# Up units of batch 0 taken by quarters of w1 over three token groups, with four moves in the loads and the fp32 bias table around them

## The chip, the cores and the metric

The kernel runs on one core of a Trainium2 chip. The time is device microseconds of one execution of the whole program, and less is better. The profile is one more execution, recorded by the hardware profiler; its times are counted from the start of its span.

## The reference

Two parts run one after the other. The first is attention over 4 batches of 8 heads, 768 positions and head dimension 64, with a bias that falls with distance, a causal window of 96 keys and 8 global keys:

```python
scores = scale * np.matmul(q, k.transpose(0, 1, 3, 2))
keep = is_global | is_local          # key < 8, or 0 <= query - key < 96
scores = np.where(keep, scores - slope[h] * dist, -1e9)
x = softmax(scores) @ v              # 4 x 768 x 512 after the heads are joined
```

The second is a mixer on x. U is 768x32, V is 32x768, w1 is 512x2048 and w2 is 2048x512:

```python
h = x.transpose(0, 2, 1) @ U @ V
u = x + h.transpose(0, 2, 1)
out = u + np.maximum(u @ w1, 0.0) @ w2
```

All inputs and the output are fp32 in memory; the kernel's matmuls take fp16, and bf16 for the bias on the tensor engine.

## The kernel before

**Work units.** Heads are taken in pairs, four pairs to a batch, so there are 16 pairs. For a pair the kernel loads q and k (`load_qk`, two transfers on the SP queue) and v (`load_v`, one), turns them to fp16 (`cast_qk`, `cast_v`, mostly on GpSimd), transposes q and k on the tensor engine (`st_T`, L239), copies the shifted keys (`st_KA`, `st_A`, `st_P`), makes the scores of three column chunks (`scores`, L339 and L346), adds the bias, takes the exponent and multiplies with v (`st_V`). A key block's scores cover two query blocks, one on the diagonal and one beside it.

**Two ways to add the bias.** For the four pairs of batch 0 (pairs 0 to 3) the tensor engine adds it, from a bf16 table `rel16` (L331), and ScalarE takes the exponent straight from PSUM (`st_SE`). From pair 4 on VectorE does it in `s_dve` (L371), from the fp32 table `relcat`, and ScalarE takes the exponent afterwards (`st_E`, L383). `relcat` is copied from `relB` by two ScalarE instructions (L733, L734), and its first eight rows are finished on GpSimd by `finish_table` (L184, L185). This stands late in the program, after pair 3's `st_V`.

**The mixer.** `st_M1` (U, L436 for batch 0) and `st_M2` (V and the identity, L453 and L458) build the transposed u in `uT`, one 128-column piece per pair. Then come up units and down units. An up unit (L582) multiplies two 128-column pieces of w1 with 256 tokens of `uT` into one PSUM bank, 8 matmuls, and ScalarE takes the relu into `htr` (L587). A batch has three token groups of 256, so 24 up units. The banks of the up units have the tag `th`, three buffers, which the transposes of `st_T` use as well. A down unit (L612) multiplies `htr` with w2.

**What sets the order.** The program is written out by hand: each engine runs its own instructions in program order. The queues `ups_q` and `downs_q` hold closures; `fill(n)` takes n units out of them at fixed places between the steps of a pair, and `unit` chooses whether an up or a down is next. `held` keeps the downs back until pair 7; by then pairs 4, 5 and 6 have taken eight up units each, all of batch 0. Before the first of them, two up units are begun with three of their four matmul pairs (`begin_up`, L502).

**The weights.** w1 is loaded by four transfers on the GpSimd queue (`load_w1`, L211), one for every 512 columns, a quarter; each casts fp32 to fp16 on the way. Up units 0 and 1 of a group need quarter 0, units 2 and 3 quarter 1, and so on. w2 follows in four more (`load_w2`, L214). U and V are loaded on the same queue during the setup (L197, L198).

**Loads of pairs.** SP issues, in this order: q and k of pairs 0 and 1, v of 0, q and k of 2, v of 1, q and k of 3, v of 2, v of 3, q and k of 4, q and k of 5, v of 4, q and k of 6, v of 5, q and k of 7, and so on. A buffer of q or k is that of the pair two before.

Of the kernel before, what the change touches and what calls it, by code (L numbers as in the profile page):

```python
# [20 lines left out]
def kernel(  # L21
# [13 lines left out]
    nc = tc.nc  # L35
# [3 lines left out]
    P = 128  # L39
# [52 lines left out]
    NVB = 4  # L92
    vbuf = [cst.tile([P, NSB, 2, D + 1], FP16, name=f"v16_{i}") for i in range(NVB)]

    def load_qk(i):
        b, h0 = i // NP, 2 * (i % NP)
        got = []
        for src, nm in ((q, "qst"), (k, "kst")):
            st = stp.tile([P, 2, NSB, D], FP32, name=nm, tag=nm, bufs=2)
            if i < NPE:  # L100
                nc.sync.dma_start(
                    st.rearrange("p h n d -> p h (n d)"),
                    src[b, h0:h0 + 2].rearrange("h (p n) d -> p h (n d)", n=NSB),
                )
            else:
                nc.sync.dma_start(
                    st.rearrange("p h n d -> p (h n) d"),
                    src[b, h0:h0 + 2].rearrange("h (n p) d -> p (h n) d", p=P),
                )
            got.append(st)  # L110
        staged[i] = got
# [82 lines left out]
    finish_table(rel16.rearrange("p a c -> p (a c)"), rel16[0:NG, :, P:])  # L194
    for t in (u16.rearrange("p n c -> p (n c)"), v16w):
        nc.gpsimd.memset(t.bitcast(I32), 0)
    nc.gpsimd.dma_start(u16[:, :, 0:R], moe_U.rearrange("(c p) r -> p c r", p=P))  # L197
    nc.gpsimd.dma_start(v16w[0:R], moe_V)  # L198
    for vt in vbuf:
        nc.gpsimd.memset(vt[:, :, :, D:D + 1], 1.0)  # L200

    w1_16 = wbig.tile([P, NDC, DFF], FP16, name="w1_16")
    w2_16 = wbig.tile([P, NJC, DM], FP16, name="w2_16")
# [333 lines left out]
    def queue_last_weight_sum():  # L537

        b12, b22 = quarters[1], quarters[3]
        for k, js in enumerate((slice(0, HJ // 2), slice(HJ // 2, HJ))):  # L540
            queue_sum("t3", k, b12[:, js], b22[:, js], b12[:, js], ALU.subtract)

    def queue_ff(b):
        for g in range(NFG):
            queue_group(b, g)

    def queue_group(b, g):
        ts = slice(g * FT, (g + 1) * FT)
# [23 lines left out]
        def mk_up(at):  # L572
            jp = at // 2 + (at % 2) * NJC // 4 if split else at

            def go():
                if jp == 0:
                    cell["htr"] = ffp.tile([P, NJC, FT], FP16, name="htr", tag="htr", bufs=3)
                hps, done = begun.pop(jp) if jp in begun else (ps_th("hps"), 0)
                for k in range(2):
                    jt = 2 * jp + k  # L580
                    for dc in range(done, NDC):
                        nc.tensor.matmul(  # L582
                            hps[:, k * FT:(k + 1) * FT],
                            w1_16[:, dc, jt * P:(jt + 1) * P], uT[:, dc, ts],
                            start=(dc == 0 and k == 0), stop=(dc == NDC - 1 and k == 1),
                        )
                nc.scalar.activation(  # L587
                    cell["htr"][:, 2 * jp:2 * jp + 2].rearrange("p j t -> p (j t)"), hps, AF.Relu
                )
                if split and at % 4 == 3:  # L590
                    queue_sums(at // 4)
            return go
# [46 lines left out]
                    store(*what)  # L639
            return go  # L640

        for at in range(NJC // 2):
            ups_q.append((mk_up(at), (b, g)))
        if split:
            x1 = mk_product("cx", lo, "a11", "b11", (n0, lo), first=True)
            x2 = mk_product("cx", lo, "s2", "t2", (n0, hi_))
# [18 lines left out]
                jobs.popleft()()  # L665

    def unit():
        down = downs_q and not held[0] and not any(w == downs_q[0][1] for _, w in ups_q)
        room = ups_q and (not downs_q or place(ups_q[0][1]) - place(downs_q[0][1])
                          < (3 if held[0] else 2))  # L670
        if down and (ahead[0] > 0 or not room):
            ahead[0] = 0
            downs_q.popleft()[0]()
        elif room:
            ahead[0] = 1
            ups_q.popleft()[0]()
# [11 lines left out]
    for i in range(NP):  # L688
        st_SE(i, 0)
        if i:  # L690
            st_V(i - 1, 0)
        cast_v(i)
        st_A(i)
        if i < 2:
            load_v(i + 2)
        if i in (1, 2):
            load_qk(NP - 1 + i)
        if i == 2:
            load_w1(0)
        if i == 3:  # L700
            load_v(NP)
        if i >= 2:
            st_M1(i - 2)
        if i:
            st_T(i + 1)
        st_SE(i, 1)
        if i:
            st_V(i - 1, 1)
        else:
            st_T(i + 1)  # L710
        st_KA(i + 1, nc.vector)
        st_P(i)
        if i == 2:
            st_M2(i - 2)
        if i == 0:
            cast_qk(i + 2, nc.vector, nc.gpsimd)
        elif i < 3:
            cast_qk(i + 2, nc.gpsimd)
        if i == 2:
            load_w1(1)  # L720
        if i == 3:
            load_w1(2)
            load_w1(3)
        st_SE(i, 2)
        if i == 3:
            st_M2(i - 2)
# [3 lines left out]
    st_V(NP - 1, 1)  # L730
    cast_qk(NP + 1, nc.gpsimd)
    st_M2(NP - 2)
    nc.scalar.copy(relcat[:, 0:512].rearrange("p (a c) -> p a c", a=2), rel3[:, 0:2])  # L733
    nc.scalar.copy(relcat[:, 512:640], relB[:, 0:P])  # L734
    finish_table(
        relcat, relcat[0:NG, 0:512].rearrange("p (a c) -> p a c", a=2)[:, :, P:]
    )
    begin_up(0, (0, 1), ps_cps("hps"))
    st_M1(NP - 1)
    begin_up(0, (2,))  # L740
# [1 line left out]
    st_M2(NP - 1)  # L742
    for xo, o, rb in later:
        nc.vector.tensor_tensor(xo, o, rb, ALU.mult)
    for hi in range(2):
        s_dve(NP, hi, first[hi])
    queue_ff(0)

    for i in range(NP, NPAIR + 2):
# [113 lines left out]
```

## Time and profile before

| what | us |
|---|---|
| median of 3 runs before | 236.97 (236.11 to 237.56) |
| the profiled execution's own time | 236.67 |
| its span, first to last instruction | 234.8 |
| VectorE busy | 151.4 (65%) |
| ScalarE busy | 112.2 (48%) |
| GpSimd busy | 80.3 (34%) |
| the SP and GpSimd queues together | 36.66 MB in 86561 packets |

In the rows that the prediction shows, PE is the tensor engine and PEld its weight loads, DVE is VectorE, ACT is ScalarE, POOL is GpSimd, and SPq is the queue from which SyncE issues transfers. A row of the timeline has the start, the time taken, the engine, the line, the operation, out<-in, the number of instructions merged into the row, and in brackets the idle time of the engine before it with what ended it. A DMA row on POOL or SPq is the issue alone; the transfer itself goes on afterwards. In a view of DMA packets by queue, q1 is the queue of SP and q0 that of GpSimd.

### The profile page before, as it was taken

How to read it: one execution, taken by the hardware profiler on the slowest of the kernel's cores; microseconds unless marked ns; L12 is line 12 of the kernel's file. 1: busy time of each engine (PE TensorE's matmuls, PEld its weight loads, DVE VectorE, ACT ScalarE, POOL GpSimd, SP SyncE). 2: the span in 40 equal slices, each digit the busy share in tenths (PEclk: the TensorE clock that was granted, in tenths of full speed). 3: DMA queues.
4: the chain of work that ended last, by engine and by line, in shares of the span. 5: the costliest groups of instructions: out<-in, count | busy, mean ns of one | idle time of the engine just before them, and what ended most of it. 6: DMA issues, size and time to landing. Idle time of an engine off the chain costs nothing.

```text
span 234.8 us, 5675 instructions
## 1 busy us (share of the span) xinstructions
PE 224.0 (95%) x2324; PEld 161.4 (69%) x2324; DVE 151.4 (65%) x349; ACT 112.2 (48%) x169; POOL 80.3 (34%) x128
## 2 busy tenths in 40 slices
PE   7989977999999999999999999999999999999994
PEld 2445755778844446876666656766688988888883
DVE  3677866468686777566667576779896543454452
ACT  6767765767714040837372626464542334334320
POOL 7379938294562432333333333302311100000000
PEclk9999999999999999999999999999999999999999
DMA  6999999999969798979695956362130302011112
GB/s 194 304 287 263 266 234 226 263 230 185 208 61 234 209 226 210 247 154 229 149 240 133 250 143 176 70 173 77 29 82 36 90 0 92 1 47 45 45 47 89
DMA packets 86561, 36.66 MB, mean 156 GB/s; under 512 B 74152, under 2 KB 83592, under 8 KB 86536
## 3 DMA queue, kind: packets, MB, share of 16 engines
q1 hardware_dynamic: 81480, 32.01, 55.6%
q0 software_dynamic: 5056, 4.29, 11.4%
q8 instruction: 18, 0.29, 0.5%
q14 instruction: 7, 0.06, 0.1%
HBM read 27.46 MB, written 6.29 MB: 144 GB/s over the span
## 4 chain that ended last, share of the span: by engine, by line
PE 77%; POOL 7%; DMA 7%; DVE 3%; ACT 1%; issue 1%; SPq 0%; POOLq 0%
PE hps L582 32%; PE cps L612 21%; PE cx L632 7%; DMA w<-in_moe_w_ch_dram 6%; PE cy L632 5%; PE sc L339 3%; PE ob L399 2%; DMA kst<-in_k_dram 2%; PE ob L395 1%; POOL v L132 1%; POOL x L419 1%; PE sc L346 1%; POOL vA L278 1%; PE tp L239 1%; POOL k L118 1%
## 5 line engine op out<-in xcount | busy, mean ns | idle before, releaser
L587 ACT ACTIVATE htr<-hps 128x512 f16<-128x512 f32 x96 | 56.9, 597 | 87.2 <-PE hps L582 84.4
L582 PE MATMUL hps<-uT,w 128*128 128x256 f16 x756 | 96.4, 273 | 2.1 <-DMA w<-in_moe_w_ch_dram 1.7
L582 PEld LDWEIGHTS <-w 128*128 128x128 f16 x756 | 70.3, 98 | 13.2 <-DMA w<-in_moe_w_ch_dram 2.2
L612 PE MATMUL cps<-w,htr 128*128 128x512 f16 x224 | 56.9, 379 | 0.0
L371 DVE SCALAR_TENSOR_TENSOR sp<-sc,relcat 128x512 f32<-128x512 f32 (+1 forms) x72 | 43.1, 641 | 19.0 <-PE sc L346 10.1
L383 ACT ACTIVATE ep<-sp 128x1408 f16<-128x1408 f32 x24 | 32.7, 1371 | 16.3 <-DVE sp L371 16.3
L612 PEld LDWEIGHTS <-htr 128*128 128x128 f16 x224 | 19.1, 97 | 16.6
L419 POOL CAST x<-x_sb 128x384 f16<-128x384 f32 x30 | 15.8, 526 | 42.2 <-DVE x_sb L418 38.8
L491 POOL CAST x<-x_sb 128x768 f16<-128x768 f32 x12 | 10.3, 856 | 49.5 <-DVE x_sb L487 49.5
L339 PEld LDWEIGHTS <-kT 64*128 64x128 f16 x192 | 8.3, 93 | 15.4 <-issue 13.4
L519 DVE TENSOR_TENSOR s<-htr 128x512 f16<-128x512 f16 x20 | 9.3, 463 | 12.7 <-ACT htr L587 12.7
L339 PE MATMUL sc<-qT,kT 64*128 64x128 f16 x192 | 16.8, 221 | 0.6 <-DVE sp L371 0.6
L418 DVE TENSOR_TENSOR x_sb<-ob,rcp 128x384 f32<-128x384 f32 x30 | 16.7, 557 | 1.0
L632 PEld LDWEIGHTS <-s 128*128 128x128 f16 x160 | 15.5, 98 | 1.9
L399 PE MATMUL ob<-v,ep 128*128 128x65 f16 x192 | 16.0, 194 | 0.0
L399 PEld LDWEIGHTS <-ep 128*128 128x128 f16 x192 | 13.7, 98 | 2.6 <-DVE x_sb L418 0.3
L346 PE MATMUL sc<-qT,kA 64*128 64x128 f16 x160 | 14.6, 217 | 0.7 <-DVE kA L270 0.3
L637 DVE TENSOR_TENSOR x_sb<-cx,x_sb 128x256 f32<-128x256 f32 x20 | 8.5, 423 | 10.1 <-PE cx L632 10.0
L132 POOL CAST v<-vst 128x768 f16<-128x768 f32 x16 | 13.4, 840 | 3.7 <-DMA vst<-in_v_dram 3.7
L358 ACT ACTIVATE ep<-sc 128x512 f16<-128x512 f32 (+1 forms) x24 | 12.1, 559 | 5.3 <-PE sc L346 4.6
L395 PE MATMUL ob<-vA,ep 128*128 128x65 f16 x160 | 14.1, 194 | 0.2 <-DVE vA L291 0.2
L632 PEld LDWEIGHTS <-htr 128*128 128x128 f16 x120 | 11.7, 98 | 1.3
(100 smaller groups left out, 267.7 us busy)
## 6 DMA issues: line engine op xcount, KB each, us to landing
qst<-in_q_dram SPq DMA_DIRECT2D x16, 384.0 KB, 5.7
kst<-in_k_dram SPq DMA_DIRECT2D x16, 384.0 KB, 5.5
vst<-in_v_dram SPq DMA_DIRECT2D x16, 384.0 KB, 6.1
out_dram<-x_sb SPq DMA_DIRECT2D x23, 256.0 KB, 2.1
w<-in_moe_w_ch_dram POOLq DMA_DIRECT2D x8, 512.0 KB, 9.8
vA<-v SPq DMA_DIRECT2D x8, 152.3 KB, 2.7
out_dram<-x_sb SPq DMA_DIRECT2D x2, 128.0 KB
uT<-x SPq DMA_TRANSPOSE x12, 2.8
```

The source lines that it names most:

```text
L339: nc.tensor.matmul(scs[hi][:, o:o + P], kT[r, kb * P:(kb + 1) * P], qT[r, kb * P:(kb + 1) * P], start=(o == 0 and not on_pe), stop=(o + P ...
L346: nc.tensor.matmul(scs[hi][:, o + P:o + 2 * P], kA[r, kb], qT[r, (kb + 1) * P:(kb + 2) * P], start=False, stop=(o + 2 * P == tot),)
L371: nc.vector.scalar_tensor_tensor(out=dst, in0=got, scalar=qk_scale / slope[2 * (i % NP) + hi], in1=relfs[c0 // 512], op0=ALU.mult, op1=ALU ...
L383: nc.scalar.activation(ep, sps.pop((i, hi)), AF.Exp, scale=slope[2 * (i % NP) + hi])
L395: nc.tensor.matmul(ob[:, qi], ep[:, OF[qi - 1]:OF[qi - 1] + P], vA[:, qi - 1, hi], start=True, stop=False,)
L399: nc.tensor.matmul(ob[:, qi], ep[:, DG[qi]:DG[qi] + P], vt[:, qi, hi], start=(qi == 0), stop=True,)
L418: nc.vector.tensor_tensor(xo, ob[:, :, 0:D], rb, ALU.mult)
L419: nc.gpsimd.tensor_copy(x16, xo)
L582: nc.tensor.matmul(hps[:, k * FT:(k + 1) * FT], w1_16[:, dc, jt * P:(jt + 1) * P], uT[:, dc, ts], start=(dc == 0 and k == 0), stop=(dc == ...
L587: nc.scalar.activation(cell["htr"][:, 2 * jp:2 * jp + 2].rearrange("p j t -> p (j t)"), hps, AF.Relu)
L612: nc.tensor.matmul(cps, htr[:, jc, t * P:(t + 1) * P], w2_16[:, jc], start=(b > 0 and jc == 0), stop=(jc == NJC - 1),)
L632: nc.tensor.matmul(ps, cell[a][:, j], tw[w][:, j], start=(first and j == 0), stop=(done is not None and j == HJ - 1), skip_group_check=True,)
```

## The change

1. The up units of batch 0 are collected over the three groups and queued by quarter of w1: two units of group 0, two of group 1, two of group 2 for quarter 0, then the same for quarters 1, 2 and 3. The condition for a down unit is widened to match. The number and the places of units stay; only which unit comes at which place changes.
2. The loads of U and V are issued after pair 0's `st_A` instead of in the setup.
3. The loads of pair 5's q and k get a write of one element by GpSimd into each of their buffers, placed behind the first `load_w1`, so that SP waits for it.
4. The fp32 table `relcat` is made in the setup, by GpSimd, and no longer by ScalarE.
5. The two `s_dve` steps of pair 4's first chunk go ahead of the last `st_M1` on VectorE; they stood behind the last `st_M2` and two products.

```diff
-    def load_qk(i):
+    def load_qk(i, behind=None):
+
         b, h0 = i // NP, 2 * (i % NP)
         got = []
         for src, nm in ((q, "qst"), (k, "kst")):
             st = stp.tile([P, 2, NSB, D], FP32, name=nm, tag=nm, bufs=2)
+            if behind is not None:
+                behind.memset(st[0:1, 0, 0, 0:1], 0.0)
...
     for t in (u16.rearrange("p n c -> p (n c)"), v16w):
         nc.gpsimd.memset(t.bitcast(I32), 0)
-    nc.gpsimd.dma_start(u16[:, :, 0:R], moe_U.rearrange("(c p) r -> p c r", p=P))
-    nc.gpsimd.dma_start(v16w[0:R], moe_V)
     for vt in vbuf:
         nc.gpsimd.memset(vt[:, :, :, D:D + 1], 1.0)
+    nc.gpsimd.tensor_copy(relcat[:, 0:512].rearrange("p (a c) -> p a c", a=2), rel3[:, 0:2])
+    nc.gpsimd.tensor_copy(relcat[:, 512:640], relB[:, 0:P])
+    finish_table(
+        relcat, relcat[0:NG, 0:512].rearrange("p (a c) -> p a c", a=2)[:, :, P:]
+    )
+
+    def load_uv():
+        nc.gpsimd.dma_start(u16[:, :, 0:R], moe_U.rearrange("(c p) r -> p c r", p=P))
+        nc.gpsimd.dma_start(v16w[0:R], moe_V)
...
+    first_ups = []
+
     def queue_ff(b):
         for g in range(NFG):
             queue_group(b, g)
+        if b == 0:
+            for c in range(4):
+                for made in first_ups:
+                    ups_q.extend(made[2 * c:2 * c + 2])
...
-        for at in range(NJC // 2):
-            ups_q.append((mk_up(at), (b, g)))
+        if b:
+            for at in range(NJC // 2):
+                ups_q.append((mk_up(at), (b, g)))
+        else:
+            first_ups.append([(mk_up(at), (b, g)) for at in range(NJC // 2)])
...
-        down = downs_q and not held[0] and not any(w == downs_q[0][1] for _, w in ups_q)
+        down = downs_q and not held[0] and not any(place(w) <= place(downs_q[0][1]) for _, w in ups_q)
...
-        if i in (1, 2):
-            load_qk(NP - 1 + i)
+        if i == 0:
+            load_uv()
+        if i == 1:
+            load_qk(NP)
         if i == 2:
             load_w1(0)
+            load_qk(NP + 1, nc.gpsimd)
...
     st_M2(NP - 2)
-    nc.scalar.copy(relcat[:, 0:512].rearrange("p (a c) -> p a c", a=2), rel3[:, 0:2])
-    nc.scalar.copy(relcat[:, 512:640], relB[:, 0:P])
-    finish_table(
-        relcat, relcat[0:NG, 0:512].rearrange("p (a c) -> p a c", a=2)[:, :, P:]
-    )
+    for hi in range(2):
+        s_dve(NP, hi, first[hi])
     begin_up(0, (0, 1), ps_cps("hps"))
     st_M1(NP - 1)
     begin_up(0, (2,))
...
     for xo, o, rb in later:
         nc.vector.tensor_tensor(xo, o, rb, ALU.mult)
-    for hi in range(2):
-        s_dve(NP, hi, first[hi])
     queue_ff(0)
```

## The prediction

> **What bounds the kernel now.** First the page: the span, the engines' shares and the costliest group of tensor matmuls. Then the DMA issues: size of each and time from issue to landing.
>
> ```profile
> span 234.8 us, 5675 instructions
> PE 224.0 (95%) x2324; PEld 161.4 (69%) x2324; DVE 151.4 (65%) x349; ACT 112.2 (48%) x169; POOL 80.3 (34%) x128
> ...
> L582 PE MATMUL hps<-uT,w 128*128 128x256 f16 x756 | 96.4, 273 | 2.1 <-DMA w<-in_moe_w_ch_dram 1.7
> ```
> ```profile
> vst<-in_v_dram SPq DMA_DIRECT2D x16, 384.0 KB, 6.1
> ...
> w<-in_moe_w_ch_dram POOLq DMA_DIRECT2D x8, 512.0 KB, 9.8
> ...
> u<-in_moe_U_dram POOLq DMA_DIRECT2D x1, 48.0 KB, 5.9
> ```
>
> The tensor engine is busy for 95%, so only what it waits for, or what keeps it from being fed, can be won. The rest is in the timeline, tensor rows first, where the up units of batch 0 begin.
>
> ```profile
> 30.43 0.61 PE L502 MATMUL hps<-uT,w 128*128 128x256 f16 x4 [0.78 <-DMA w<-in_moe_w_ch_dram]
> ...
> 33.23 0.38 PE L582 MATMUL hps<-uT,w 128*128 128x256 f16 x2 [0.32 <-DVE uT L464]
> ...
> 34.76 0.21 PE L339 MATMUL sc<-qT,kT 64*128 64x128 f16 x1 [0.26 <-DVE sp L371]
> ...
> 35.35 0.21 PE L339 MATMUL sc<-qT,kT 64*128 64x128 f16 x1 [0.39 <-DVE sp L371]
> ...
> 38.17 1.92 PE L582 MATMUL hps<-uT,w 128*128 128x256 f16 x16 [0.31 <-DMA w<-in_moe_w_ch_dram]
> ...
> 41.52 1.92 PE L582 MATMUL hps<-uT,w 128*128 128x256 f16 x16 [1.43 <-DMA w<-in_moe_w_ch_dram]
> ...
> 45.26 0.50 PE L239 MATMUL tp<-ident,k 128*128 128x128 f16 x6
> ```
>
> Read the brackets: units 5 and 7 wait for quarters 2 and 3 of w1 (0.31 and 1.43 us), pair 4's second chunk waits for the bias steps that empty its score banks (0.26 and 0.39). A wait costs more than its bracket. Sixteen matmuls take 1.92, one alone 0.273, so one follows another after (1.92 - 0.273)/15 = 0.11, and each restart loses 0.273 - 0.11 = 0.16 of overlap.
>
> **Quarters of w1: -2.06.** With three groups sharing a quarter, quarter 1 is first needed by the seventh unit instead of the third, quarter 2 by the thirteenth. The waits at 38.17 and 41.52 go: 0.31 + 1.43 + 2 x 0.16 = 2.06. The units are the same in number, place and shape.
>
> **Pair 4's bias steps sooner: -0.97 and +0.15.** The rows on VectorE:
>
> ```profile
> 29.73 0.55 DVE L464 CAST uT<-ups 128x384 f16<-128x384 f32 x1
> 31.41 0.29 DVE L440 CAST tmp<-tmp_ps 128x128 f16<-128x128 f32 x1 [1.14 <-PE tmp_ps L436]
> ...
> 34.02 1.28 DVE L371 SCALAR_TENSOR_TENSOR sp<-sc,relcat 128x512 f32<-128x512 f32 x2
> ```
>
> The two steps run from 30.28 to 31.56 in what is idle time, and the score banks are free three microseconds before they are wanted: 0.26 + 0.39 + 2 x 0.16 = 0.97 saved. But the tmp copy now stands behind them and starts at 31.56 instead of 31.41, and the last uT piece and the unit at 33.23 hang on it: +0.15. For the same reason the 0.78 at 30.43 gives nothing if quarter 0 comes sooner: VectorE is next in line there.
>
> **The table on GpSimd, U and V later, about 0.** GpSimd's early rows, with two of the tensor engine:
>
> ```profile
> 5.04 1.04 POOL L197 DMA_DIRECT2D u<-in_moe_U_dram  x1
> 6.08 0.53 POOL L198 DMA_DIRECT2D v16w<-in_moe_V_dram  x1
> ...
> 10.61 0.84 POOL L132 CAST v<-vst 128x768 f16<-128x768 f32 x1 [3.68 <-DMA vst<-in_v_dram]
> 11.51 0.84 POOL L278 COPY vA<-v 128x650 f16<-128x650 f16 x1
> 13.32 0.83 POOL L118 CAST k<-kst 128x768 f16<-128x768 f32 x1 [0.97 <-ACT ep L358]
> ```
> ```profile
> 17.94 0.50 PE L436 MATMUL tmp_ps<-x,u 128*128 128x128 f16 x6
> ...
> 19.08 0.51 PE L239 MATMUL tp<-ident,k 128*128 128x128 f16 x6 [0.26 <-POOL k L118]
> ```
> ```profile
> q0 software_dynamic: 812, 0.10, 50.3%
> ```
>
> The table's two copies have 640 elements, fewer than the 768 of a 0.84 us cast, and each of the four steps is taken at no more than 0.84: at most 3.4. The cover is the 3.68 idle plus the 1.57 that the two issues leave free. Without that cover it would delay pair 0's v by up to 3.4. The Trainium skill, GPSIMD Engine Reference, section Instruction dispatch, says that a freshly loaded routine's first call costs about 6 us more; by that the copies would overrun the cover by 2 us or more. The first cast (0.84, at 10.61) and the first copy (0.84) show nothing like it. ScalarE loses two copies where it idles: nothing.
>
> The issues of U and V now take 1.57 between 12.35 (end of the vA copy) and pair 2's k cast, where 0.97 is idle: +0.60 if v lands as now. Against that, the last row, packets from 7.9 to 11, is theirs: 50.3% of 3.1 us is 1.56 us of all DMA engines, which now falls behind v and pair 2. If all of it reaches v, that cast is up to 0.96 sooner, but the tensor engine can use only what it waits there, 0.4 by the like row at 19.08 (0.26 + 0.16). Ends -0.4 and +0.6; I take 0. U is first used at 17.94; 12.35 + 5.9 is 18.25, and the wait at 19.08 (0.26 + 0.16) absorbs delays up to 18.36: 0.
>
> **Pair 5 behind quarter 0, and what it does to pair 4's v: +1.0 with the relus.** The queue shares are the packets of 28 to 32, of 33 to 38, and what is left of w1 after 40. The next two fences show how long a first issue on an idle queue takes to move packets: issued at 0.74, six packets by 1.9.
>
> ```profile
> q0 software_dynamic: 431, 0.43, 63.0%
> q1 hardware_dynamic: 431, 0.63, 51.8%
> ```
> ```profile
> q0 software_dynamic: 774, 0.77, 90.3%
> q1 hardware_dynamic: 773, 0.20, 30.0%
> ```
> ```profile
> q0 software_dynamic: 50, 0.04, 12.0%
> ```
> ```profile
> DMA packets 6, 0.01 MB, mean 5 GB/s; under 512 B 0, under 2 KB 6, under 8 KB 6
> ```
> ```profile
> 0.74 0.46 SPq L101 DMA_DIRECT2D qst<-in_q_dram  x1
> ...
> 18.95 0.42 SPq L101 DMA_DIRECT2D qst<-in_q_dram  x1
> ```
> ```profile
> 21.02 0.79 POOL L211 DMA_DIRECT2D w<-in_moe_w_ch_dram  x1
> ...
> 37.16 0.84 POOL L132 CAST v<-vst 128x768 f16<-128x768 f32 x1
> ...
> 38.74 0.83 POOL L118 CAST q<-qst 128x768 f16<-128x768 f32 x1
> ...
> 40.35 1.57 POOL L214 DMA_DIRECT2D w<-in_moe_w_ch_dram  x2
> ...
> 46.84 0.72 POOL L269 COPY kA<-kT 128x640 f16<-128x640 f16 x1 [0.35 <-DVE kT L262]
> ```
>
> When both queues have work they alternate packet for packet: 431 to 431, 774 to 773. By the bytes per packet a quarter of w1 is 512 packets, q and k of a pair 512 together, v 1536. Now q of pair 5 is issued at 18.95; afterwards it waits for 21.02 + 0.79 and the two one-element writes (at most 0.2 on GpSimd, in the range only): 22.0. Packets start about 1.2 later, as at the program's start: 23.2. Beside w1 at 431/4 = 108 packets per us they need 4.75, to 28.0, and pair 4's v, behind them in SP's queue, meets quarters 1 to 3, also 1536 packets: at 774/5 = 155 per us it takes 9.9, to 37.9. That is a mean over 16 engines. After 40.0 a tenth of quarter 3 was left (50 of 512), and unit 7 got it at 41.52, so the slowest engine comes some 1.5 behind; I allow 1.8, an estimate. The rows above put v's cast at 37.16 today, so v becomes what is late next, and behind its wait on GpSimd are queued the vA copy, pair 6's q and k and the issue of w2 (first used by the downs of pair 7, so late w2 costs nothing yet). On SP the q and k of pair 6 and v of pair 5 follow v of pair 4 and come later with it. From 37.9 to 39.7 the chain 0.84 + 0.84 + 2 x 0.83 + 1.57, then pair 4's x cast (384 elements, half of a 0.84), 5.33 in all, ends at 43.2 to 45.0; there stands the kA copy, at 46.84 now, and from it the chain goes on to the tensor engine. So at the late end only 1.84 of the 2.88 is left there, and 1.04 is given back.
>
> The relus give back too. The rows on ScalarE:
>
> ```profile
> 33.64 0.60 ACT L587 ACTIVATE htr<-hps 128x512 f16<-128x512 f32 x1 [0.22 <-PE hps L582]
> 34.14 0.79 ACT L261 COPY qT<-tp 128x768 f16<-128x768 f16 x1
> ...
> 39.75 1.37 ACT L383 ACTIVATE ep<-sp 128x1408 f16<-128x1408 f32 x1
> ```
>
> Pair 6's transposes of k, at 45.26, need the bank that relu 8 frees. From 33.64 ScalarE has eight relus, one copy and two exponents: 4.8 + 0.79 + 2.74 = 8.33, to 41.97, and about 0.8 of idle stays, as units 3 to 5 come 0.88 apart (8 x 0.11) and a relu takes 0.60: 42.8. The tensor engine would be there at 45.26 - 2.88 = 42.38. So 0.4 is lost, 0.3 more at the next unit: 0.7, at the same place as the 1.04 and not on top of it. I take 1.0, near the v end, since the last of 16 engines decides a landing.
>
> **Sum.** -2.06 - 0.97 + 0.15 + 1.0 = -1.88, against the profiled execution's own 236.67: 234.8. That execution is 0.3 below the median of the runs, 236.97; the forecast is 0.9% below that median. A measurement of this kernel can tell about 1% from no change: the bounds are 234.6 and 239.3.
>
> **Rivals.** *v arrives in time.* Quarter 0 starts later than pair 5, so v meets fewer of its packets, and the first pairs gain the 0.4. Then only the relus give back: -2.88 + 0.7 - 0.4 = -2.58, 234.1. For it: SP's queue has nothing ahead of pair 5. Against: the alternation in the fences. 0.36.
>
> *v much later.* From 39.7 on each further microsecond is lost whole; at 41.0 it is 1.3 more, 236.1. For it: the slowest engine. 0.12.
>
> *U comes late, slower.* U is moved into DMA traffic; w's transfers take 9.8 where U took 5.9. At 9.8, U lands at 22.15 and the first `st_M1` at 17.94 stops all tensor work behind it: 22.15 - 18.36 = 3.8, to 238.6. It costs from 18.36 on and makes the kernel slower than before from 20.2. For it: both pass the same queue. Against: U has a tenth of the bytes, and its packets alternate. 0.08. The Trainium skill, DMA: Bandwidth & Descriptors, section Anatomy of one DMA — SWDGE (gpsimd) path, gives about 2.0 us plus the bytes at 436 GB/s; for U that makes an estimate of 2.1, which would end this rival; the row's 5.9 differs, and the row is used.
>
> *The table overruns its cover*, by a first call on GpSimd far above the 0.84 rows: 5.25 of cover, and what is more goes to pair 0's v; 2 us more would be 236.8. 0.02.
>
> **Numbers.** The forecast has 0.42. Faster by over 1%: the first rival and a fifth of the forecast, 0.45. Slower: the upper half of the U rival, and sums that go wrong in several terms, 0.07. Between: 0.48. The range: below, the full 3.03 and the early 0.4 with nothing given back, 233.2; above, the late v's 236.1 with the 0.6 and 0.2 on GpSimd, 236.9; the U rival is left out.
>
> **What would show it.** Right: no bracket on w behind the first, none on sp at pair 4's second chunk; v's cast at 38 to 40 with a wait for its transfer; the kA copy at 44.5 to 45.5. Wrong: a wait on u at 17.9, brackets on v's copy or on pair 6's transposes above 1 us, or a new wait on w2.

## The result, and the profile after

| | median of the runs | lowest and highest |
|---|---|---|
| before | 236.89 us (20 runs) | 235.1 to 238.24 |
| changed | 235.41 us (20 runs) | 234.34 to 237.55 |

The ratio is 0.9944, with a 95% interval of 0.9923 to 0.9964: 0.6% faster. A ratio here is taken over the runs within 1.5% of the fastest of their kernel, and is not the quotient of the two medians, which hold every run. The forecast was 234.8, with a range of 233.2 to 236.9.

The profiled execution is the slowest of the 20, 237.55. So the changed kernel was run and profiled once more (after_again, 235.60), and both profiles are read below. One run of an experiment (split_no_hold, its profiled one) took 780.5 us, with the up units' matmuls at 696 ns instead of 273; nothing is read from that profile. First the page of the profiled execution: the span, and the group of the up units' matmuls with their idle time.

```profile
span 235.7 us, 5676 instructions
...
L598 PE MATMUL hps<-uT,w 128*128 128x256 f16 x756 | 96.2, 273 | 0.5 <-DVE uT L474 0.3
```

The up units (L582 before, L598 now) wait 0.5 us in all where they waited 2.1, and the wait is no longer for w. The next rows are the changed kernel's timeline on the tensor engine, at the places of the prediction and at those that it did not foresee.

```profile
14.87 0.51 PE L249 MATMUL tp<-ident,k 128*128 128x128 f16 x6 [1.31 <-POOL k L121]
...
24.68 0.23 PE L356 MATMUL sc<-qT,kA 64*128 64x128 f16 x2 [1.14 <-DVE kA L280]
...
33.30 0.34 PE L463 MATMUL ups<-v16w,tmp 128*128 128x384 f16 x1 [0.33 <-DVE tmp L450]
...
36.20 1.91 PE L598 MATMUL hps<-uT,w 128*128 128x256 f16 x16 [0.16 <-ACT qT L271]
38.04 0.23 PE L349 MATMUL sc<-qT,kT 64*128 64x128 f16 x2
...
38.31 3.67 PE L598 MATMUL hps<-uT,w 128*128 128x256 f16 x32
...
72.41 0.32 PE L438 MATMUL ob<-u,x 128*128 128x32 f16 x6 [1.74 <-POOL x L429]
```

From 36 to 42 the up units run through: sixteen matmuls in 1.91, thirty-two in 3.67, with no bracket for w. The two brackets on sp are gone as well. In their place stand five others: k of pair 2 at 14.87 (before: 0.50 us at 14.20), a shifted-key copy at 24.68, the tmp copy at 33.30, a short one on ScalarE's qT copy at 36.20, and x at 72.41.

To see what each place costs, the start of the same tensor instruction was taken from each trace, and the start in the profile of before subtracted. Where the figure falls from one row to the next, that stretch gained; where it rises, it lost.

| start before, us | what lies ahead of it | after_again | changed, slowest run | quarters_only | uv_late |
|---|---|---|---|---|---|
| 12.72 | the start | -0.10 | -0.14 | +0.35 | +0.09 |
| 14.33 | k of pair 2 | +0.69 | +0.67 | +0.40 | +0.88 |
| 21.99 | pairs 2 and 3 | +0.71 | +0.66 | +0.40 | +0.88 |
| 23.76 | small copies of pairs 2 and 3 | +1.50 | +1.65 | +0.39 | +0.88 |
| 29.10 | pair 4's k, last `st_V` | +1.49 | +1.57 | +0.39 | +0.88 |
| 30.93 | quarter 0 of w1 | +0.54 | +0.61 | +0.33 | +1.19 |
| 32.69 | tmp copy | +1.15 | +1.22 | +0.33 | +1.19 |
| 36.22 | pair 4's second chunk | +0.45 | +0.52 | +0.33 | +1.19 |
| 42.84 | quarters 1 to 3 of w1 | -1.53 | -1.46 | -1.65 | +1.19 |
| 46.68 | pair 6's transposes, relus | -1.15 | -1.07 | -1.26 | +1.19 |
| 68.28 | pairs 6 and 7 | -1.09 | -1.00 | -1.19 | +1.19 |
| 71.62 | x ahead of pair 6's `st_M1` | -1.08 | **+0.92** | -1.19 | +1.18 |
| 229.79 | the rest | -1.09 | +0.92 | -1.19 | +1.18 |

After 72 nothing changes any more. The second profile gives -1.09 at the end, and the medians differ by 1.48. The slowest run lost 1.92 in one place, at 72.

### The profile page after: what moved, and what is told of

Read it like the earlier page. It is cut to its first block, busy times and chain, and to the rows that moved or that the text cites. A ratio compares the mean times of both kernels' runs of the same rounds, so it can differ in the third digit from the quotient of the medians.

```text
span 235.7 us, 5676 instructions
## 1 busy us (share of the span) xinstructions
PE 224.1 (95%) x2324; PEld 161.3 (68%) x2324; DVE 152.5 (65%) x349; ACT 111.3 (47%) x167; POOL 81.0 (34%) x132
## 4 chain that ended last, share of the span: by engine, by line
PE 73%; POOL 7%; DMA 6%; DVE 6%; SPq 2%; ACT 2%; issue 2%; DVEq 0%; POOLq 0%
PE hps L598 29%; PE cps L628 19%; PE cx L648 7%; DMA vst<-in_v_dram 6%; PE cy L648 5%; PE sc L349 3%; PE ob L409 2%; POOL v L135 2%; POOL vA L288 2%; PE ob L405 1%; DVE sp L381 1%; SPq L109 1%; PE sc L356 1%; ACT ep L393 1%; ACT htr L603 1%
## 5 line engine op out<-in xcount | busy, mean ns | idle before, releaser
L598 PE MATMUL hps<-uT,w 128*128 128x256 f16 x756 | 96.2, 273 | 0.5 <-DVE uT L474 0.3
L598 PEld LDWEIGHTS <-w 128*128 128x128 f16 x756 | 70.5, 98 | 11.4 <-issue 0.4
L628 PEld LDWEIGHTS <-htr 128*128 128x128 f16 x224 | 19.1, 97 | 16.6
L121 POOL CAST k<-kst 128x768 f16<-128x768 f32 x14 | 11.6, 830 | 5.1 <-DMA kst<-in_k_dram 5.1
```

Source lines behind the costliest of these rows:

```text
L598: nc.tensor.matmul(hps[:, k * FT:(k + 1) * FT], w1_16[:, dc, jt * P:(jt + 1) * P], uT[:, dc, ts], start=(dc == 0 and k == 0), stop=(dc == ...
L628: nc.tensor.matmul(cps, htr[:, jc, t * P:(t + 1) * P], w2_16[:, jc], start=(b > 0 and jc == 0), stop=(jc == NJC - 1),)
```

## The experiments

| run | edit | median (runs) | before, same chip | ratio, 95% interval | profiled execution | tensor engine at the end |
|---|---|---|---|---|---|---|
| after_again | none | 235.56 (10) | 236.71 | 0.9956 [0.992, 0.9992] | 235.60 | -1.09 |
| no_hold | pair 5 not held | 235.08 (12) | 236.71 | 0.9925 [0.990, 0.995] | 235.63 | -1.02 |
| uv_setup | U, V in the setup | 235.17 (12) | 236.71 | 0.9934 [0.9907, 0.9961] | 234.32 | -2.27 |
| no_hold_uv | both | 235.15 (12) | 236.71 | 0.9923 [0.9896, 0.995] | 234.03 | -2.61 |
| quarters_only | before + quarters | 235.17 (12) | 236.61 | 0.996 [0.9936, 0.9984] | 235.46 | -1.19 |
| port_split | uv_setup + two moves | 234.95 (12) | 236.61 | 0.9956 [0.9926, 0.9985] | 235.62 | -0.98 |
| no_hold_warm | no_hold + filler | 235.07 (12) | 236.61 | 0.9958 [0.9927, 0.9988] | 234.69 | -1.90 |
| split_no_hold | no_hold_uv + one move | 234.81 (7) | 237.12 | 0.9905 [0.9867, 0.9943] | 780.5 | none |
| w1_sooner | split_no_hold + w1 sooner | 233.36 (6) | 237.12 | 0.9853 [0.9811, 0.9894] | 232.58 | -4.00 |
| uv_late | before + U, V later | 237.09 (12) | 236.68 | 1.0031 [1.0, 1.0061] | 237.74 | +1.18 |
| split_again | as split_no_hold | 234.25 (12) | 236.68 | 0.9918 [0.9885, 0.9951] | 233.63 | -2.92 |
| w1_sooner_again | as w1_sooner | 233.87 (6) | 236.68 | 0.9891 [0.9854, 0.9928] | 235.06 | -1.53 |

The runs of one kernel spread over 1 to 2 us, so most of these ratios cannot be put in order among themselves. What tells the terms apart is the place in the trace where the tensor engine gains or loses; the last column is that of the one profiled execution, which can lie over 1 us from the median of its kernel (no_hold_uv, w1_sooner_again).

### The changed kernel once more

> The changed kernel once more, for a second profile. In its first profile the tensor engine is 1.0 us ahead of before from 45 to 70 us and then loses 1.9 at 72.4, where the first matmul of pair 6's U product waits for GpSimd, which waits for pair 7's v (landed at 70.2). That execution took 237.55, the median of 20 is 235.41. Theory A, the loss at 72.4 belongs to some executions only: this profile shows a wait under 0.5 us there and a time near 235.4. Theory B, it is in every execution: again more than 1.2 us there, and the early part must then gain as much more in the median. Ratio to before 0.994 (0.991 to 0.997) by both.

Without a new edit the loss at 72 was not there, and the earlier losses were. The rows are the second profile's, tensor engine and then GpSimd:

```profile
23.92 0.23 PE L356 MATMUL sc<-qT,kA 64*128 64x128 f16 x2 [0.33 <-DVE kA L280]
...
24.80 0.19 PE L405 MATMUL ob<-vA,ep 128*128 128x65 f16 x1 [0.45 <-DVE vA L301]
...
67.47 0.84 POOL L135 CAST v<-vst 128x768 f16<-128x768 f32 x1 [1.18 <-DMA vst<-in_v_dram]
```

Pair 7's v was cast at 67.47, in time for the `st_M1` that needs what GpSimd does behind it. So the 1.74 at 72.41 belongs to some executions only; the losses at 14 and 24 came in both.

### Pair 5 not held

```diff
-            load_qk(NP + 1, nc.gpsimd)
+            load_qk(NP + 1)
```

> The changed kernel without the two one-element writes: pair 5's q and k go out when their buffers are free, as before. Theory A, the hold makes pair 4's v and pair 6's q and k late and so gives time back: v's cast near 37 with no wait, pair 6's casts without waits (0.84 and 1.20 in the changed kernel's profile), the kA copy of pair 6 near 45.1 instead of 45.85, later loads some 1.5 us earlier; time 0.5 to 1.0 less than the changed kernel, ratio to before 0.989 to 0.992. Rival, the hold is what takes away the waits for w1: quarter 0 lands 2 to 3 us later and the tensor engine waits for it up to 1.5 us at the begun units; time 236 or more, ratio 0.996 or higher.

Pair 4's v is cast at 37.48 here without a wait, and still the tensor engine loses 0.39 between 42.84 and 46.68, as with the hold (0.38 and 0.39). So the late v cost the tensor engine nothing there. ScalarE's relus did, by the order of the rows; these are ScalarE and then the tensor engine in the changed kernel's slowest run:

```profile
43.38 1.09 ACT L603 ACTIVATE htr<-hps 128x512 f16<-128x512 f32 x2
```
```profile
43.47 0.50 PE L249 MATMUL tp<-ident,q 128*128 128x128 f16 x6
44.04 0.49 PE L249 MATMUL tp<-ident,k 128*128 128x128 f16 x6
44.53 1.03 PE L598 MATMUL hps<-uT,w 128*128 128x256 f16 x8
```

The transposes of k start 0.57 behind those of q (0.34 in before), about where the first of the two relus ends, and the unit stands 0.49 behind them (0.33 in before), where the second ends: 0.39 together.

The rival falls too. From 29.10 to 30.93 no_hold gains the same 0.95 as after_again, without the hold: quarter 0 landed at 30.66 by the trace, and the tensor engine, 1.55 late by then, came after it. In the changed kernel the hold, with quarter 0 landed at 27.23, saved no wait.

What the hold did cost is at 24: from 21.99 to 23.76 no_hold loses 0.19 (1.38 to 1.57), after_again 0.79. But this profile lost 1.34 between 14.3 and 16.2. The windows of no_hold show why. The columns are the window, its length, the busy time of PE, PEld, DVE, ACT and POOL, and then the granted clock of the tensor engine, the DMA share and GB/s:

```profile
14.00:15.00 1.00, 0.43 (x7) 0.43 (x8) 0.00 (x0) 0.16 (x1) 1.00 (x3) 0.91 1.20 297
15.00:18.50 3.50, 3.50 (x32) 1.57 (x31) 2.04 (x5) 1.18 (x3) 1.76 (x3) 0.54 1.21 194
```

After the 1.30 us wait for k of pair 2 the clock fell to one half, and stayed there for 3.41 us by the trace (14.82 to 18.23). By the medians, no_hold is 0.5 below after_again, with intervals that overlap.

### U and V back in the setup

```diff
+    nc.gpsimd.dma_start(u16[:, :, 0:R], moe_U.rearrange("(c p) r -> p c r", p=P))
+    nc.gpsimd.dma_start(v16w[0:R], moe_V)
...
-        if i == 0:
-            load_uv()
```

> The changed kernel with U and V loaded in the setup again. Theory A, their issues on GpSimd (1.81 us in the profile) delay pair 2's k cast and cost the tensor engine 0.67 net: the wait before pair 2's k transposes falls from 1.3 to about 0.5, time 0.4 to 0.7 less, ratio 0.991 to 0.993. Rival, U and V then take DMA time from pairs 0 to 2 as before and the two cancel: ratio as the changed kernel, 0.994.

> Both undone: what is left is the order by quarters, the table on GpSimd and the bias steps sooner. Theory A: the two gains add, 1.0 to 1.7 less than the changed kernel, ratio 0.987 to 0.990, and only the relus' queue limits the stage of pair 4 (waits for relus of some 0.5 us). Rival: the waits for quarter 0 of w1 come back, ratio 0.994 or higher.

With U and V in the setup the tensor engine stands at -0.64 behind k of pair 2 (uv_setup) and at -0.25 (no_hold_uv), against +0.69 in after_again; counted from 12.72, where they stand at -0.42, -0.02 and -0.10, the first two gain 0.2 and after_again loses 0.79. The loss at 24 stays in uv_setup, which keeps the hold (from -0.64 to +0.39), and is not there in no_hold_uv (-0.25, -0.20). So they are two causes. In no_hold_uv, where the tensor engine is early, the 0.60 wait for quarter 0 of w1 is back, as its rival had it. The medians do not add up as the theory wanted: 235.08, 235.17 and, with both undone, 235.15. The -2.61 of no_hold_uv belongs to an execution of 234.03.

### Quarters alone

> The kernel before with the order by quarters alone. Theory (the prediction's first term): the waits for w at 38.17 and 41.52 go (0.31 + 1.43 + 2 x 0.16 = 2.06), the 0.78 wait for quarter 0 at 30.43 and the 0.26 and 0.39 waits for the bias steps stay, and the relus give back about 0.4 at pair 6's transposes, as they did in the four profiles so far. So the tensor engine stands 2.06 earlier than before at the unit of 42.8 and 1.6 earlier from 47 on; about 1.6 us, ratio 0.993. Rival (the waits for w hide each other, and quarter 2 or 3 is late again somewhere later): a wait for w stays and the gain is below 1, ratio above 0.996.

The edit is the first item of the change on the kernel before. The rows are its tensor engine where before had 0.31 and 1.43:

```profile
36.00 1.92 PE L588 MATMUL hps<-uT,w 128*128 128x256 f16 x16
...
38.12 3.67 PE L588 MATMUL hps<-uT,w 128*128 128x256 f16 x32
```

Both waits are gone. The table shows +0.33 to -1.65, which is 1.98, and 0.39 given back behind it: the term of 2.06 and that of the relus, each by itself. The rival fell. Its ratio, 0.996, is that of the whole change within the intervals, and its profile ends at -1.19 beside the -1.09 of after_again: the other four moves together gave nothing that these show.

### U and V later, alone

```diff
+        if i == 0:
+            load_uv()
```

> The kernel before with one edit: U and V are issued behind pair 0's vA copy instead of at the start. The prediction took 0 for this (ends -0.4 and +0.6). Theory from the profiles so far: the two issues take 1.8 of GpSimd between that copy and pair 2's k cast, which starts at 13.9 to 14.1 instead of 13.32; the tensor engine's wait ahead of pair 2's transposes of k grows from 0.50 to 1.2 to 1.3, 0.7 to 0.8 later; U lands at 18.3 to 19.1, and 0.4 comes back at pair 3's transposes of k (the 0.26 wait at 19.08) where U does not come too late. At the end 0.3 to 0.8 later than before: median 237.2, ratio 1.002. Rival (the prediction's): v of pair 0 comes 0.9 sooner without U and V ahead of it and makes room for the issues; the wait stays at 0.5 and the end at 0 +- 0.1.

First the tensor engine's row of before, then GpSimd's and the tensor engine's of uv_late:

```profile
14.20 0.51 PE L239 MATMUL tp<-ident,k 128*128 128x128 f16 x6 [0.50 <-POOL k L118]
```

```profile
10.76 0.84 POOL L132 CAST v<-vst 128x768 f16<-128x768 f32 x1 [5.43 <-DMA vst<-in_v_dram]
...
12.38 1.29 POOL L198 DMA_DIRECT2D u<-in_moe_U_dram  x1
13.67 0.53 POOL L199 DMA_DIRECT2D v16w<-in_moe_V_dram  x1
14.20 0.84 POOL L118 CAST k<-kst 128x768 f16<-128x768 f32 x1
...
15.09 0.51 PE L241 MATMUL tp<-ident,k 128*128 128x128 f16 x6 [1.30 <-POOL k L118]
```

The k cast stands right behind the issues, at 14.20 instead of 13.32, and the tensor engine's wait grows from 0.50 to 1.30, which is 0.79 in the table. Pair 0's v is not sooner (10.76, 10.61 before), although nothing of U and V is ahead of it. The 0.4 that was to come back at 19 did not: that wait is for GpSimd too (0.26 still), and moves with it. In this profile the wait for quarter 0 is longer besides (1.09 for 0.78). By the medians it costs 0.4, by the ratio 0.7, with an interval from nothing to 1.4 us.

### GpSimd's casts and VectorE's small copies

port_split starts from uv_setup. Two copies at i = 2 go from VectorE to ScalarE (that of `st_P` also moves behind the pair's last exponents, left out here), and the second bias step goes behind the last `st_M1`:

```diff
-        eng.tensor_copy(
+        small = nc.scalar.copy if i == 3 else eng.tensor_copy
+        small(
             kA[:, 1:, 0:NG], kT[:, 0:NG].unsqueeze(1).broadcast_to((P, NSB - 2, NG))
...
-    for hi in range(2):
-        s_dve(NP, hi, first[hi])
+    s_dve(NP, 0, first[0])
     begin_up(0, (0, 1), ps_cps("hps"))
     st_M1(NP - 1)
+    s_dve(NP, 1, first[1])
```

> Starts from uv_setup (U and V issued at the start, the hold kept) with two edits. First, the two small copies that VectorE makes between GpSimd's casts at 21 to 23.3 (32 elements into kA of pair 3, 8 x 520 into vA of pair 2) go to ScalarE. Theory: VectorE's copy took 1.98 because it had to wait for GpSimd's casts to end; on ScalarE it takes under 0.5 whatever GpSimd does, the 1.19 wait of the tensor engine for kA at 23.42 becomes 0.5 or less, and the tensor engine is 0.7 to 1.0 earlier there than in uv_setup. Rival: the copy is slow by its data or by the transfers of w1 that run then; ScalarE's takes over 1 us as well and nothing is gained. Second, pair 4's second bias step is moved behind the tmp copy: the 0.33 wait for tmp (loss 0.49) goes, so between 30.9 and 34.1 the tensor engine no longer loses 0.61 against before but about 0.1. Sum 1.2 to 1.5 earlier than uv_setup, if w1's quarter 0 is not the next in line (it landed at 27.2 in the changed kernel): span about 231.2, median about 234.0, ratio 0.988. If quarter 0 or the relus take it, a wait for w stands at the first up unit and the median stays at 235.

First the changed kernel's VectorE and GpSimd at the place, from the slowest run:

```profile
22.64 1.98 DVE L280 COPY kA<-kT 128x32 f16<-128x32 f16 x1
24.53 0.28 DVE L301 COPY vA<-v 8x520 f16<-8x520 f16 x1
```
```profile
22.55 0.50 POOL L429 CAST x<-x_sb 128x384 f16<-128x384 f32 x1
23.00 0.82 POOL L121 CAST q<-qst 128x768 f16<-128x768 f32 x1
23.77 0.82 POOL L121 CAST k<-kst 128x768 f16<-128x768 f32 x1
```

The copy of 32 elements starts 0.09 behind the x cast and ends at 24.62, with the end of the k cast (24.59): it stood through three casts. In uv_setup it took 1.98 again, in after_again 1.21 (to the end of the q cast), in before and in no_hold 0.40 (to the end of the x cast). Now the same copies on ScalarE, and the tensor engine behind them, in port_split:

```profile
21.72 0.22 ACT L279 COPY kA<-kT 128x32 f16<-128x32 f16 x1 [0.55 <-DVE kA L277]
...
22.60 0.61 ACT L301 COPY vA<-v 8x520 f16<-8x520 f16 x1
```
```profile
23.25 0.19 PE L405 MATMUL ob<-vA,ep 128*128 128x65 f16 x1 [0.44 <-ACT vA L301]
...
70.51 0.32 PE L438 MATMUL ob<-u,x 128*128 128x32 f16 x6 [1.51 <-POOL x L429]
```

On ScalarE the copy takes 0.22 beside the same casts, and the stretch loses 0.27 (-0.31 to -0.04) where uv_setup lost 1.03. The rival (slow by its data or by w1's transfers) falls. The Trainium skill says in "SBUF — State Buffer", section "SBUF: two separate sides", that a pair of ports shared by GpSimd and a VectorE instruction in a two-port mode is an exclusive lock: the one that starts first has it for its whole instruction, and the other is blocked. The trace agrees with the blocking, though no run shows the mode, and it shows more: the copy was blocked for up to three instructions on end.

The second move worked too: between 30.93 and 32.69 port_split loses 0.10, the changed kernel 0.61. Yet the sum did not arrive. From 42.84 to 46.68 it gives back 0.93, this time with waits of 0.12 and 0.46 for GpSimd's q and k casts of pair 6, and at 70.5 it loses 1.68, the same wait for x as in the slowest run of the changed kernel.

### Is the spread of the runs the clock?

no_hold_warm puts five idle matmuls of zeros, extra work, between pair 2's transposes of q and k:

```diff
         for st in (stq, stk):
+            if i == 2 and st is stk:
+                warm(5)
```

> no_hold with five idle matmuls of zeros (0.21 each at full clock, 1.07 in all) between pair 2's transposes of q and of k, where the tensor engine waited 1.30 for the k cast. They are extra work and change no result. Theory (a window of about 3.4 us that is only half busy drops the clock, and this makes the slow runs of no_hold): the window 11.2 to 14.6 is now 0.78 busy instead of 0.47 and no execution drops the clock; the median falls from 235.08 to about 234.4 and no run lies above 235.0. Rival (the drop was a single accident, and the spread has another source, such as the moment at which the full clock begins at the start): the median stays at 235.1 +- 0.3 and the runs spread from 234.2 to 235.8 as before.

The windows of no_hold_warm at the place:

```profile
14.00:15.00 1.00, 0.78 (x6) 0.21 (x4) 0.00 (x0) 0.48 (x1) 1.00 (x3) 1.00 0.89 292
15.00:18.50 3.50, 3.34 (x51) 1.78 (x51) 2.49 (x6) 1.97 (x5) 2.78 (x5) 1.00 1.39 232
```

The clock stays full in this execution. But the median is 235.07 against 235.08, and the runs spread from 234.12 to 237.09: the theory that such drops make the spread fell. The mean granted clock of every run says how much of it they make. Half a clock for 3.41 of 234 us lowers the mean by 0.007, and three of the 12 runs of no_hold have 0.991 or 0.992, at 235.42, 235.63 and 235.77. The other nine, at 0.997 to 1.0, still spread from 234.16 to 235.50. In no_hold_warm one run has 0.992, the slowest (237.09), so a drop of that size can stand somewhere in an execution in spite of the filler. Runs with a drop are among the slower ones, but most of the spread is there without one, and what makes it stays open.

This profile, without the hold and without a drop, also prices the hold once more: from 21.99 to 23.76 it loses nothing, and at the end it stands 0.81 ahead of after_again.

### What the wait at 72 hangs on

split_no_hold is no_hold_uv with the move of the second bias step. w1_sooner issues quarter 0 sooner on top of that:

```diff
-        if i == 2:
-            load_w1(0)
...
+        if i == 1:
+            load_w1(0)
         if i == 2:
             load_w1(1)
```

> port_split without its hold: pair 5's q and k are issued as in the kernel before, the two small copies are back on VectorE, U and V at the start, the tmp copy ahead of the second bias step. Theory (the hold leaves the DMA engines short of work from 22 to 26, 163 GB/s in port_split and 105 in the changed kernel where the kernel before moved 280, and all later transfers are that much later, w2 and pair 7's v with them): 22 to 26 is back at 250 to 280 GB/s, pair 7's v lands at 64 to 65.5 instead of 68.31, the 1.51 wait before M1 at 70.5 is gone, and pair 4's v and pair 6's q and k no longer make GpSimd wait. In exchange quarter 0 of w1 comes later: a wait of 0.6 to 0.8 for w at the first up unit. VectorE's two small copies take 0.4 and 0.96. The tensor engine is 2.6 to 3.1 earlier than before from 47 to the end, 2.0 more than port_split at the end; median about 234.3. Rival (the wait at 70.5 comes from the tensor engine being early, whatever the hold): v lands at 67 or later here too and 1.5 is lost at 70.5.

> split_no_hold with w1's quarter 0 issued two microseconds sooner on GpSimd: behind pair 3's k cast (18.8) instead of behind pair 2's vA copy (20.8). Nothing is held, so the DMA engines stay full. Theory: quarter 0 lands at 27 to 28.5 instead of 30.0 and the 0.6 to 0.8 wait at the first up unit (loss 0.77) goes; pair 4's and 5's q and k, which share the engines with it, land up to 1.5 later and have that much room; x, v and vA of pair 2 are 0.79 later on GpSimd, and VectorE's vA copy at 22 to 23 waits for that by 0.3 at most. The tensor engine is 3.2 to 3.6 earlier than before at the end: span 231.3, median about 233.6, ratio 0.987, the best of all. Rival: pair 4's k lands at 23 or later and its transposes wait, or the vA copy of pair 2 comes late at 23: a wait of 0.7 or more takes the place of the one for w, and the median is that of split_no_hold.

> split_no_hold once more, since its profile was of a disturbed execution of 780 us. Theory as there: 250 to 280 GB/s from 22 to 26, pair 7's v lands at 64 to 65.5, no wait at 70.5, a 0.6 to 0.8 wait for w at the first up unit; the tensor engine 2.6 to 3.1 earlier than before at the end, median 234.3. Rival as there: v lands at 67 or later and 1.5 is lost at 70.5.

> w1_sooner once more, beside split_again on the same chip, with more runs. Theory: 0.9 to 1.4 faster than split_again (its 0.77 for w, and what the early rows gave), median 233.3, ratio 0.985 to 0.987. Rival (six runs were too few): the two agree within 0.4.

The windows from 22 to 26, of before, of the slowest run of the changed kernel, and of split_again:

```profile
22.00:26.00 4.00, 3.83 (x66) 2.54 (x62) 3.93 (x9) 3.24 (x6) 3.69 (x6) 1.00 1.11 280
```
```profile
22.00:26.00 4.00, 2.86 (x47) 1.77 (x45) 3.93 (x8) 2.01 (x5) 3.29 (x7) 1.00 0.75 105
```
```profile
22.00:26.00 4.00, 3.77 (x66) 2.54 (x66) 3.90 (x10) 3.28 (x7) 3.63 (x6) 1.00 1.15 268
```

The hold left the DMA engines 105 GB/s where before had 280: 0.7 MB of (280 - 105) x 4 us that come later. Without it the stretch is full again. GpSimd in split_again:

```profile
35.58 0.84 POOL L135 CAST v<-vst 128x768 f16<-128x768 f32 x1
...
65.21 0.84 POOL L135 CAST v<-vst 128x768 f16<-128x768 f32 x1 [0.75 <-DMA vst<-in_v_dram]
```

Pair 7's v is cast at 65.21 instead of 67.5 to 70.3, and nothing waits at 70. The 0.37 for quarter 0 at the first up unit is what stays. The theory held, with -2.92 at the end and a median of 234.25.

w1_sooner was the fastest of the three kernels on its chip, with no wait for w and -4.00 at the end. Its repeat shows that the hold is not needed for the wait at 70: GpSimd and the tensor engine of w1_sooner_again.

```profile
37.82 0.84 POOL L135 CAST v<-vst 128x768 f16<-128x768 f32 x1 [2.97 <-DMA vst<-in_v_dram]
...
41.61 1.48 POOL L222 DMA_DIRECT2D w<-in_moe_w_ch_dram  x2
...
67.80 0.84 POOL L135 CAST v<-vst 128x768 f16<-128x768 f32 x1 [3.74 <-DMA vst<-in_v_dram]
```
```profile
69.95 0.32 PE L436 MATMUL ob<-u,x 128*128 128x32 f16 x6 [1.60 <-POOL x L427]
```

Put beside each other, the profiles with a wait at 70 to 72 have one thing in common: pair 4's v was not there when GpSimd wanted it.

| profile | pair 4's v cast, wait | pair 7's v cast, wait | wait for x at pair 6's `st_M1` |
|---|---|---|---|
| before | 37.16, none | 67.31, none | none |
| uv_setup | 36.23, none | 65.22, none | none |
| split_again | 35.58, none | 65.21, 0.75 | none |
| w1_sooner | 34.49, none | 63.96, 0.58 | none |
| no_hold | 37.48, none | 66.30, none | none |
| no_hold_uv | 35.89, none | 64.99, 0.23 | none |
| no_hold_warm | 36.60, none | 65.41, none | none |
| quarters_only | 37.49, none | 66.13, none | none |
| uv_late | 38.35, none | 68.50, none | none |
| after_again | 38.30, 0.82 | 67.47, 1.18 | none |
| changed, slowest run | 38.17, 0.62 | 70.26, 3.88 | 1.74 |
| port_split | 38.72, 3.43 | 68.36, 3.65 | 1.51 |
| w1_sooner_again | 37.82, 2.97 | 67.80, 3.74 | 1.60 |

By the traces pair 4's v landed at 34.31 to 38.66 in the four profiles with the hold, and at 25.55 to 30.89 in those without, but for w1_sooner_again (37.77). With the hold it was still in time in uv_setup. Where v is late, pair 6's casts stand behind it and w2's first issue behind those: 41.61 in w1_sooner_again, 37.68 in w1_sooner. By the trace w2's last quarter lands at 61.43 instead of 58.01, and what SP queues behind, pair 8's k, the transposes of u and pair 7's v, follows. The tensor engine then waits if it is early enough itself: after_again, with pair 4's v as late, is 1.6 us later there than port_split (-1.09 and -2.66 at 68.28) and did not wait. That does not explain the two profiles of the changed kernel. Pair 4's v was cast at 38.17 and 38.30 and the tensor engine stood at -1.00 and -1.09, yet w2's last quarter landed at 63.32 in the slowest run and at 62.28 in after_again, and pair 7's v at 70.21 and 67.41. What sets these two apart is open. The order of events is shown by the traces; that pair 4's v is the cause and not a companion was not tested by an edit of v alone. split_again and w1_sooner_again differ by 0.38 in the median, within the 0.4 of the rival, split_no_hold and w1_sooner by 1.45; two sets of six runs of w1_sooner do not settle how much the sooner issue is worth, and one of its two profiles loses it again at 70. Their medians, 234.25 and 233.87 in the last set of runs, are below the changed kernel's 235.41, but it did not run beside them, and only the first set of w1_sooner has an interval (0.9811 to 0.9894) clear of the changed kernel's.

## Why the prediction was right

The time was within its range and the sign was right, but the total came out near by errors of both signs, which is luck in part. Against -1.88 stands -1.09 in after_again, and -1.48 between the medians. Its terms, each from the table:

- **Quarters, -2.06.** Measured 1.98 in after_again and in quarters_only. Right in mechanism and size.
- **Bias steps sooner, -0.97 and +0.15, nothing for quarter 0.** The brackets on sp went, but a 0.16 wait for ScalarE's qT copy followed at 36.20: -0.70. Quarter 0 did give its wait back, -0.95 (in no_hold as well, since the tensor engine came late), and the tmp copy cost 0.61, not 0.15: once the tensor engine does not wait at 30.43, the same two steps stand in front of a tmp copy that is wanted sooner. The prediction saw that VectorE is next in line and priced it against the old start. The sum of these, -1.04, is near the predicted -0.82.
- **Relus and v, +1.0.** The relus were forecast at 0.7 and measured 0.38. The transfers went as worked out: pair 5's q and k landed at 28.53 and 29.56 (28.0 was the sum), and pair 4's v at 38.12 (37.9 for the mean, 39.7 for the last engine). It was cast at 38.17 with a wait, as forecast (38 to 40), so "v arrives in time" is out, and the kA copy of pair 6 stood at 45.85, 0.35 past the forecast's 44.5 to 45.5. But its price was nothing, since no_hold gives back the same 0.39. The step that failed is "So at the late end only 1.84 of the 2.88 is left there": the tensor engine came there 1.5 earlier than before, not 2.88, and did not yet need the end of the chain. In port_split, 2.3 earlier still, the chain and the relus did cost 0.93.
- **Table on GpSimd, 0.** Right. Pair 0's v was cast at 10.56 with a 3.74 wait for its transfer; the table was hidden.
- **U and V later, 0.** Wrong by 0.79. "If all of it reaches v, that cast is up to 0.96 sooner" was the step: v came no sooner at all, so the two issues, 1.81 us in this kernel, pushed k of pair 2 whole. The upper end, +0.6, was also too low by 0.2, because it took the issues at their 1.57 of before; 1.81 less the idle 0.97 is 0.84.
- **The hold on GpSimd, at most 0.2.** Measured 0.79, and 0.99 in the slowest run, where no_hold loses 0.19 and no_hold_warm nothing. It is not the time of the two writes. It comes through VectorE's small copies, which stood through up to three of GpSimd's casts; with these copies on ScalarE, port_split loses 0.27 although it keeps the hold. The prediction weighed GpSimd's work by GpSimd's queue only. Why the copies wait longer with the hold is not shown: the 32-element copy starts 0.08 to 0.09 us behind the x cast with it, and 0.15 to 0.16 behind in before, no_hold, no_hold_uv and split_again.
- **U late.** The rival asked for a wait on u. There was one of 0.34 in after_again at 19.13, and none in the other profile; at 22 nothing was left of it. From issue to landing U took 6.1 us by the slowest run's trace and 6.9 by after_again's, not the estimate of 2.1 by the Trainium skill's formula ("DMA: Bandwidth & Descriptors", section "Anatomy of one DMA — SWDGE (gpsimd) path"): the row of before, 5.9, was the nearer one.

The measured terms of the quarters, of pair 4 with quarter 0, and of the relus make -1.98 - 1.04 + 0.38 = -2.64; the two of 0.79, the -0.10 from the first twelve microseconds and the places between bring it to -1.09. no_hold_uv, without either of the two, ends at -2.61, though not by the same sum: its quarter 0 gives back 0.17 and its tmp copy costs nothing.

What the prediction did not see at all is pair 7's v. It followed the hold to pair 4's v and stopped at "late w2 costs nothing yet". That w2 itself was late cost nothing, for no wait on w2 stands in the profiles; pair 7's v, which landed after it, cost 1.92 in the slowest run.

## What to carry to other kernels

A wait that is put into a queue to let one transfer pass can leave the DMA engines short of work, here down to 105 GB/s for four microseconds, and what stands behind it comes late: pair 4's v was late in three of the four profiles with the hold. Issuing the wanted transfer sooner also took away the wait for quarter 0, without the hole; one of its two profiles had the late v all the same. When work on GpSimd is moved, look at what VectorE does at the new time, not only at GpSimd's own queue. And when one wait is removed, price the next in line against the new start of its engine, not against the old.

## What the runs showed of the hardware that was not expected

- A VectorE copy of 128x32 between buffers in SBUF took 0.40, 1.21 or 1.98 us; the long ones ended with the second or third of GpSimd's casts in a row. On ScalarE it took 0.22.
- The tensor engine's clock fell to one half for 3.41 us in no_hold after a wait of only 1.30 us. In the 3.41 us ahead of the drop (11.40 to 14.82) the records of the tensor engine cover 0.47 of the time. The Trainium skill, "TensorE: Matmul & The Clock Gate", section "What's actually happening", gives a window of 3413 ns, which agrees with the length, and a slow clock after at least one idle window; here a window that was half busy was enough. In the changed kernel's profiles the same wait brought no drop. Counted in steps of 3.41 us from the start of the full clock (4.58 us in no_hold, 5.62 in after_again, 6.48 in the slowest run), the step that holds the wait is 0.47 busy in no_hold, 0.60 in after_again and 0.62 in the slowest run; in no_hold it also holds a 0.51 wait before 11.89. The same section of the Trainium skill says that the window runs freely of the kernel. The trace agrees so far, as the full clock starts between 4.5 and 7.2 us in the 13 profiles. That the busy share of a step decides is inferred from these three.
- One kernel took two courses: pair 4's v landed at 30.9 in w1_sooner and at 37.8 in its repeat, and the program was the same.
